# Attention and a gated feed-forward layer: other PSUM banks behind an attention burst, and two sums and one row sum in other places

## The chip, the cores and the metric

The kernel runs on one core of a Trainium2 chip. The metric is the device time of one execution in microseconds (us). The engines are called as the profile calls them: PE (TensorE: matmuls; its weight loads are listed as PEld), DVE (VectorE), ACT (ScalarE), POOL (GpSimd) and SP (which issues most transfers).

## The reference

Attention runs within chunks of 64 tokens, and its output is the input of a gated feed-forward layer:

```python
scores = scale * np.matmul(q_c, k_c.transpose(0, 1, 2, 4, 3))
scores = scores - np.max(scores, axis=-1, keepdims=True)
attn = np.exp(scores)
attn = attn / (np.sum(attn, axis=-1, keepdims=True) + 1e-09)
out = np.matmul(attn, v_c)
...
x = np.ascontiguousarray(attn_out.transpose(0, 2, 1, 3)).reshape(B * S, H * D)
g = x @ w_gate
silu = g * (1.0 / (1.0 + np.exp(-g)))
val = x @ w_val
return (silu * val @ w_out).astype(np.float32)
```

There are 8 batches, 8 heads, 576 tokens and head size 64, so x is 4608 x 512; w_gate and w_val are 512 x 1536, w_out is 1536 x 512. All arrays are float32.

## The kernel before

The 4608 tokens are nine blocks of 512. Three blocks are worked off one by one while the weights are prepared. The other six go in three pairs of blocks (`for b in range(3, NB, 2)` at the end of the function), and the change touches these pairs alone. Each float32 operand is held as a rounded upper part and a remainder, so a product of two operands is three matmuls.

**A pair** has two stages. The first is `gated_steps`: twelve steps, one for each 128 columns of the hidden layer (f = 0 to 11). Instead of eight block products a step takes seven (`seventh`, i = 0 to 6) of prepared sums of x and of weights, each 6 matmuls of 128x128 by 128x512. They go to three PSUM banks: `ps1` takes products 0, 2, 4 and 6 one on top of the other, `ps2` takes 1 and 5, `ps3` takes 3. ACT copies ps1 and ps2 out after products 0, 1 and 2 (to `h`, `v2`, `v1`), DVE adds later states of the banks to them (`add(h, ps3)`, `add(v2, ps1)` after product 4, `add(v1, ps2)`), ACT applies Silu, DVE multiplies. `Left` splits the result for the output product. Product 6 may only start when `add(v2, ps1)` has read ps1, since it adds to the same bank; the Silu of `h2` reads ps1 after product 6. Between products 5 and 6 stand the matmuls of `turns`: the output product of the step before, in four parts of 2, 1, 2 and 1 matmuls.

**The second stage** is `seven_products`: 15 units k of 12 matmuls that multiply sums of the hidden rows by sums of w_out. Before each unit, `before_unit(k)` issues on ACT the rounding of a sum (`U(k)`, line 1337) and on DVE the remainder (`L(k)`, line 1341); PE's unit k waits for them. DVE also finishes output blocks there (`finish`, lines 1399 and 1388) and works on the next pair's x (`n.s1`, `n.s4`, `n.s2`, lines 1173, 1180 and 1184, and `XL`, line 1353).

**Bursts.** While a pair runs, the attention of the next pair's two blocks is done inside its steps: at the end of steps 1 and 5 the scores of one block (`scores`, 64x64 matmuls, line 324), of steps 8 and 10 the products with v (`cross`, line 409). A burst fills four banks, two of pool `ps_gv` and then two of pool `ps_a`. The last pair has no next one and no bursts.

**Banks.** `ps_a` and `ps_gv` have two banks each, handed out in turn: a new tile gets the bank that was handed out the longest time ago and waits for its last reader. `ps_o` has four, which hold the pair's output products. In a step of the kernel before, ps1 is of `ps_a`, ps2 and ps3 are of `ps_gv`.

**Order.** PE, ACT and DVE run their instructions in the order in which the code is written; each takes the next only when what it waits for is there. Semaphores are set by the framework.

Lines behind a name are those of the kernel before.

Of the kernel before, what the change touches and what calls it, by code (L numbers as in the profile page):

```python
# [8 lines left out]
F32 = mybir.dt.float32  # L9
# [8 lines left out]
P = 128  # L18
# [6 lines left out]
NF = DF // P  # L25
# [8 lines left out]
def attn_then_gated_ffn(ctx: ExitStack, tc: tile.TileContext, qk, v, wgv, wo, out):  # L34
# [36 lines left out]
    def put_back(ps):  # L71
        return ps.rearrange("p (b a) -> p a b", a=2)

    def in_halves(x):
        return x.rearrange("p (a b) -> p a b", a=2)
# [602 lines left out]
    class Couple:  # L678
# [63 lines left out]
        def U(self, q):  # L742
            upper(self.a, self.bank(2, None), q)
# [380 lines left out]
    def scores(a, beside_pair=True, at=None, tiles=None, first=0):  # L1124

        if not tiles:
            tiles = [a.load_qk(0, 2, const, at)] if at else [a.load_qk(0), a.load_qk(1)], [a.load_qk(2, 2, const, a.at)]
        if first:
            ps2 = a.products(tiles[1], pool=ps_gv, tag="ps_gv")
            ps = a.products(tiles[0]), ps2  # L1130
        elif beside_pair:
            ps = a.products(tiles[0]), a.products(tiles[1], pool=ps_gv, tag="ps_gv")
        else:
            ps = a.products(tiles[0], pool=ps_gv, tag="ps_gv"), a.products(tiles[1])
        s = a.take(ps[0], 0)
        if beside_pair:
            a.less_top(ps[1], 2)
        a.less_top(s, 0)
        if not beside_pair:
            a.less_top(ps[1], 2)  # L1140
# [275 lines left out]
    def gated_steps(pair, middle, mid, behind, bursts, nothing=lambda: None):  # L1416
        for f in range(NF):
            for g in range(f + (f > 0), min(f + 2, NF)):
                w = hp.tile([P, 2, HM], F32R, name="left", tag=("h", "o_sb")[g % 2])
                nc.sync.dma_start(out=w.bitcast(F32), in_=two_o[g // 2][:, g % 2, :, :HM])  # L1420
                lefts[g] = w
            ps1 = ps_a.tile([P, N], F32, name="ps_a", tag="ps_a")
            ps2 = ps_gv.tile([P, N], F32, name="ps_gv")
            ps3 = ps_gv.tile([P, N], F32, name="ps_gv")
            h, h2 = pair.row(0, f), pair.row(1, f)
            v12 = const.tile([P, 2, N], F32, name="v", tag=("ts", "wo1")[f % 2])
            v1, v2 = v12[:, 0], v12[:, 1]
            seventh(ps1, pair.x, loaded[f], 0, True)
            nc.scalar.copy(out=in_halves(h), in_=put_back(ps1))
            seventh(ps2, pair.x, loaded[f], 1, True)  # L1430
            nc.scalar.copy(out=in_halves(v2), in_=put_back(ps2))
            seventh(ps1, pair.x, loaded[f], 2, False)
            nc.scalar.copy(out=in_halves(v1), in_=put_back(ps1))
            middle.get(f, nothing)()
            if f == NF - 1:
                pair.upper(1)
                pair.lower(1)
            seventh(ps3, pair.x, loaded[f], 3, True)
            if f not in value_first:
                add(h, ps3)  # L1440
            seventh(ps1, pair.x, loaded[f], 4, False)
            add(v2, ps1)
            if f in value_first:
                add(h, ps3)
            nc.scalar.activation(h, h, AF.Silu, scale=2.0 ** -8)  # L1445
            seventh(ps2, pair.x, loaded[f], 5, False)
            add(v1, ps2)
            times(h, v1)
            left = Left(pair, f, h, lefts[f])
            mid.get(f, nothing)()  # L1450
            left.lower()
            turns([0] if f in bursts else range(T))
            if f == NF - 1:
                pair.s2_of(0)
            seventh(ps1, pair.x, loaded[f], 6, False)
            nc.scalar.activation(in_halves(h2), put_back(ps1), AF.Silu, scale=2.0 ** -8)  # L1456
            times(h2, v2)
            if f in bursts:
                ahead_of_burst = [1] if f < 8 else []
                turns(ahead_of_burst)  # L1460
                bursts[f]()
                turns([t for t in (1, 2, 3) if t not in ahead_of_burst])
            behind.get(f, nothing)()
            for at, what, j in ((8, pair.s3, 0), (8, pair.s3, 1), (9, pair.s1_of, 0), (10, pair.s1_of, 1), (10, pair.s3, 2)):
                if f == at:
                    what(j)
            pending.append((left, None))
            if f + 2 < NF:
                load_weights(f + 2)
            elif f == NF - 2:  # L1470
                pair.load_sums(0)
                pair.load_sums(1)
                pair.upper(0)
                pair.lower(0)
            else:
                pair.load_sums(2)
                pair.load_sums(3)

    def seven_products(pair, n):

        loaded.clear()
        ps1, ps3 = pair.banks[0], pair.banks[1]
        ps2 = [ps_gv.tile([P, N], F32, name="ps_gv") for _ in range(2)]
        c22 = const.tile([P, 2, N], F32, name="c", tag="ts")
        c12 = const.tile([P, 2, N], F32, name="c", tag="wo1")
        c11 = [hp.tile([P, N], F32, name="c", tag="o_sb") for _ in range(2)]
# [31 lines left out]
        def before_unit(k):  # L1518
            if k == 0:
                pair.s1_of(2)  # L1520
                U(2), pair.s2_of(1), L(2), U(3), pair.s2_of(2), L(3)
            elif k == 1:
                U(4), pair.s4_of(0), L(4)
            elif k == 2:
                U(5), pair.s4_of(1), L(5)
                each(snapshot, c11, ps1)
            elif k == 3:
                U(6), pair.s4_of(2), L(6)
                each(finish(0, 0), c11, ps3)
            elif k == 4:  # L1530
                each(snapshot, c22, ps2)
                U(7), L(7), XU(0), call("s1")
            elif k == 5:
                U(8), L(8), XL(0), XU(1), call("s4")
            elif k == 6:
                each(snapshot, c12, ps1)
                U(9), L(9), call("s2"), XL(1)
            elif k == 7:
                U(10), L(10), XU(2)
            elif k == 8:  # L1540
                U(11), L(11), XL(2), XU(6)
            elif k == 9:
                U(12)
                each(finish(0, 1), c12, ps2)
                L(12)
            elif k == 10:
                U(13), L(13), XL(6)
            elif k == 11:
                U(14), XU(3), L(14), XL(3)
            elif k == 12:  # L1550
                each(snapshot, c21, ps1)
                XU(4)
                each(finish(1, 1), c22, ps1)
                call("s5"), XL(4)
# [134 lines left out]
    for b in range(3, NB, 2):  # L1689
        n, middle, mid, behind, bursts = None, {}, {}, {}, {}  # L1690
        if b + 2 < NB:
# [6 lines left out]
            def behind_factors(f, what):  # L1698
                with tc.issue_after(given[f]):
# [1 line left out]

            bursts = {1: lambda: scores(c, tiles=(q0, q2), first=2), 5: lambda: behind_factors(5, lambda: scores(n.second(), first=2)),
                      8: lambda: cross(c, first=2), 10: lambda: cross(n.a[1], first=2)}
            middle = {2: lambda: c.exponents(0, NP), 6: lambda: n.a[1].exponents(0, NP)}
            mid = {3: turned(c, 0, 1), 4: turned(c, 3, 1), 5: turned(c, 6, 1), 6: turned(c, 7, 1),
                   7: lambda: turn_some(n.a[1], 0, 1), 8: lambda: turn_some(n.a[1], 2, 1), 9: lambda: turn_some(n.a[1], 5, 1)}
            behind = {2: lambda: c.normalize(0, NP), 3: turned(c, 1, 2), 4: turned(c, 4, 2),
# [44 lines left out]
```

## Time and profile before

| what | value |
| --- | --- |
| median of 3 runs | 845.51 us (844.75 to 846.48) |
| the profiled execution | 845.21 us, of which the span from first to last instruction is 843.3 us |
| PE busy | 822.9 us, 98% of the span |
| DVE busy | 656.0 us, 78% |
| ACT busy | 438.1 us, 52% |
| POOL busy | 100.7 us, 12% |
| DMA | 217.51 MB, mean 258 GB/s |
| first pair, from 318.77 to 498.37 us | 179.60 us |
| second pair, from 498.37 to 675.77 us | 177.40 us |
| third pair, from 675.77 to the end | 167.53 us |

Times in the profile are us from the span's start. A row of a timeline is one instruction or a run of equal ones (xN), with its start and how long it lasts; in brackets stand how long the engine had been idle before it and who ended that. Matmuls overlap in the pipeline, so a run's duration reaches some tenths of a us into the next row; the distance between starts is the pace.

### The profile page before, as it was taken

To read this page: it belongs to the slowest core of one execution; us is meant where nothing else is said; L and a number is where in the kernel's file an instruction comes from. 1 tells how busy PE (TensorE), PEld (TensorE's weight loads), DVE (VectorE), ACT (ScalarE), POOL (GpSimd) and SP (SyncE) were. 2 spreads that over 40 slices of the span, in tenths; PEclk is the share of its full clock that TensorE was granted. 3 is DMA by queue.
4 is the path that set the end of the run, shared out by engine and by line. 5 is a ranking of instruction groups with operands and counts; after the bars stand their busy time and mean duration, and the time that the engine had idled before them with its cause. 6 is when DMAs were issued, how large, how long until landed. Compare 5 with 4: busy or idle time off the path is not lost.

```text
span 843.3 us, 14878 instructions
## 1 busy us (share of the span) xinstructions
PE 822.9 (98%) x5910; PEld 707.5 (84%) x5910; DVE 656.0 (78%) x944; ACT 438.1 (52%) x600; POOL 100.7 (12%) x94
## 2 busy tenths in 40 slices
PE   7999999999999999999999999999999999999998
PEld 5788788788888888888888888888878788888887
DVE  5987989867788774798997996888969963435696
ACT  4978899862614344635425644435445633333462
POOL 2100000000057673414300000000000000000000
PEclk9999999999999999999999999999999999999999
DMA  9967679799899796699976786687646866656563
GB/s 325 342 258 267 249 260 358 296 347 341 291 373 372 229 322 227 223 331 288 302 232 231 242 281 195 235 282 229 197 165 232 285 199 203 199 208 208 205 209 80
DMA packets 126949, 217.51 MB, mean 258 GB/s; under 512 B 56736, under 2 KB 88096, under 8 KB 116896
## 3 DMA queue, kind: packets, MB, share of 16 engines
q1 hardware_dynamic: 124560, 213.68, 74.3%
q10 hardware_dynamic: 2320, 2.88, 1.0%
q8 instruction: 47, 0.77, 0.4%
q14 instruction: 22, 0.18, 0.1%
HBM read 166.72 MB, written 49.81 MB: 257 GB/s over the span
## 4 chain that ended last, share of the span: by engine, by line
PE 68%; DVE 16%; DMA 6%; ACT 5%; issue 3%; SPq 1%; DVEq 0%; ACTq 0%
PE ps_a L933 21%; PE ps_gv L933 15%; PE ps_o L1298 10%; PE ps_gv L518 9%; DMA raw<-in_wgv 4%; PE ps_o L586 3%; PE ps_o L587 3%; PE ps_o L588 3%; DVE halves L1341 2%; PE ps_gv L1298 2%; DVE turned L396 2%; PE ps_a L324 2%; DMA w<-w 2%; DVE rows L1315 1%; PE ps_a L409 1%
## 5 line engine op out<-in xcount | busy, mean ns | idle before, releaser
L933 PE MATMUL ps_a<-x,factors 128*128 128x512 f32 x864 | 206.8, 380 | 2.7 <-ACT halves L1337 1.5
L933 PEld LDWEIGHTS ps_a<-x,factors 128*128 128x128 f32 x864 | 162.5, 189 | 28.3 <-DVE v L938 2.4
L933 PE MATMUL ps_gv<-x,factors 128*128 128x512 f32 x648 | 157.7, 379 | 0.0
L933 PEld LDWEIGHTS ps_gv<-x,factors 128*128 128x128 f32 x648 | 122.3, 189 | 17.8 <-DVE s_sb L340 0.5
L518 PE MATMUL ps_gv<-xh,w 128*128 128x512 f32 x320 | 94.0, 380 | 0.2 <-DVE w L157 0.2
L396 DVE STREAM_TRANSPOSE turned<-s_sb 32x256 f32<-32x256 f32 x192 | 83.6, 436 | 2.7
L1298 PE MATMUL ps_o<-halves,sums 128*128 128x512 f32 (+1 forms) x324 | 70.5, 375 | 3.0 <-PE ps_o L1298 1.8
L1298 PEld LDWEIGHTS ps_o<-halves,sums 128*128 128x128 f32 x324 | 59.7, 189 | 12.9 <-DVE halves L1341 2.8
L518 PEld LDWEIGHTS ps_gv<-xh,w 128*128 128x128 f32 x320 | 60.3, 189 | 8.9 <-DVE w L157 0.5
L557 DVE SCALAR_TENSOR_TENSOR rows<-v,rows 128x512 f32<-128x512 f32 x72 | 52.1, 723 | 14.2 <-ACT rows L1456 5.3
L1445 ACT ACTIVATE rows<-rows 128x512 f32<-128x512 f32 x36 | 22.7, 632 | 77.6 <-DVE rows L938 77.6
L518 PE MATMUL ps_gv<-xl,w 128*128 128x512 f32 x160 | 59.2, 383 | 1.3 <-ACT h L550 0.7
L1298 PE MATMUL ps_o<-hh,left 128*128 128x512 f32 x216 | 55.3, 383 | 0.0
L1280 ACT CAST hh<-rows 128x512 fp32r<-128x512 f32 x36 | 22.3, 618 | 63.4 <-DVE rows L557 63.4
L586 PE MATMUL ps_o<-both,hh 128*128 128x512 f32 (+1 forms) x151 | 55.0, 372 | 0.0
L587 PE MATMUL ps_o<-both,hh 128*128 128x512 f32 x144 | 54.6, 379 | 0.0
L588 PE MATMUL ps_o<-both,hh 128*128 128x512 f32 x144 | 54.6, 379 | 0.0
L938 DVE TENSOR_TENSOR rows<-rows,ps_gv 128x512 f32<-128x512 f32 x36 | 24.6, 683 | 37.1 <-PE ps_gv L933 36.9
L1341 DVE TENSOR_TENSOR halves<-rows,halves 128x1024 fp32r<-128x1024 f32 x36 | 43.0, 1215 | 10.4 <-ACT halves L1337 10.1
L938 DVE TENSOR_TENSOR v<-v,ps_a 128x512 f32<-128x512 f32 x44 | 30.1, 684 | 23.6 <-PE ps_a L933 23.6
L1298 PE MATMUL ps_gv<-halves,sums 128*128 128x512 f32 x216 | 48.1, 379 | 0.0
L1337 ACT CAST halves<-rows 128x1024 fp32r<-128x1024 f32 x36 | 37.1, 1049 | 19.0 <-DVE rows L1315 9.4
(171 smaller groups left out, 1391.1 us busy)
## 6 DMA issues: line engine op xcount, KB each, us to landing
factors<-t SPq DMA_DIRECT2D x36, 1024.0 KB, 6.9
factors<-w SPq DMA_DIRECT2D x36, 512.0 KB, 4.4
w<-w SPq DMA_DIRECT2D x16, 1024.0 KB, 7.8
sums<-s SPq DMA_DIRECT2D x15, 1024.0 KB, 4.9
qk_t<-in_qk SPq DMA_DIRECT2D x26, 512.0 KB, 7.9
t<-th SPq DMA_DIRECT2D x24, 512.0 KB, 4.0
raw<-in_wgv SPq DMA_DIRECT2D x11, 1024.0 KB, 6.8
both<-o SPq DMA_DIRECT2D x22, 512.0 KB, 6.3
```

Of the source, the lines that this page charges most:

```text
L396: nc.vector.transpose(out=self.turned[to:to + 32, p:p + 2, j, :, 32 * (i % 2):32 * (i % 2) + 32], in_=src[32 * i:32 * i + 32, :, o // 2, 3 ...
L518: nc.tensor.matmul(ps, w, by_turns(x), start=first and (k, i) == which[0], stop=last and (k, i) == which[-1])
L557: nc.vector.scalar_tensor_tensor(out=h, in0=v, scalar=2.0 ** -8, in1=h, op0=ALU.mult, op1=ALU.mult)
L586: nc.tensor.matmul(o[:, at], hl[:, ts], by_turns(woh)[:, at.start // 2:at.stop // 2], start=f == a.steps[0], stop=False)
L587: nc.tensor.matmul(o, hh[:, ts], by_turns(wol), start=False, stop=False)
L588: nc.tensor.matmul(o, hh[:, ts], by_turns(woh), start=False, stop=f == a.steps[1])
L933: nc.tensor.matmul(ps, w[u][:, k], by_turns(x[i][v][:, k]), start=first and k == 0 and n == 0, stop=k == NK // 2 - 1 and n == 2, skip_grou ...
L938: nc.vector.tensor_tensor(out=t, in0=t, in1=put_back(ps), op=ALU.add)
L1298: nc.tensor.matmul(to, w[:, i, u], by_turns(a[:, at]), start=first and n == 0, stop=n == 2, skip_group_check=True)
L1337: nc.scalar.copy(out=t[:, 0], in_=src)
L1341: nc.vector.tensor_tensor(out=lo, in0=src, in1=hi.bitcast(F32), op=ALU.subtract)
L1445: nc.scalar.activation(h, h, AF.Silu, scale=2.0 ** -8)
```

## The change

Four things change, all in the three pairs.

1. In a step behind a burst (f = 2, 6, 9 and 11 of the first two pairs) ps1 and ps2 come from `ps_gv` and ps3 from `ps_a`. In the first two pairs the units 0 to 2 and 6 to 8 of the second stage use `ps_a` instead of `ps_gv`.
2. In the bursts with scores, ACT copies the two `ps_gv` banks out (they are filled first) and DVE subtracts the maxima straight from the two `ps_a` banks; before it was the other way round.
3. `n.s1` and `n.s4`, the first two sums for the next pair's x, leave `before_unit(4)` and `before_unit(5)` and go to step 11, behind ACT's copy to `v1`; `U(1)` goes one place forward on ACT there.
4. `s1_of(0)`, a sum of rows, leaves the end of step 9 and goes into step 10, ahead of `left.lower()`. In steps 8 and 10 the second part of `turns` goes ahead of the burst.

```diff
@@ scores
+        if first:
+            s = a.take(ps[1], 2)
+            a.less_top(ps[0], 0)
+            a.less_top(s, 2)
+            return
         s = a.take(ps[0], 0)
@@ gated_steps
-            ps1 = ps_a.tile([P, N], F32, name="ps_a", tag="ps_a")
-            ps2 = ps_gv.tile([P, N], F32, name="ps_gv")
-            ps3 = ps_gv.tile([P, N], F32, name="ps_gv")
+            banks = (lambda: ps_a.tile([P, N], F32, name="ps_a", tag="ps_a")), (lambda: ps_gv.tile([P, N], F32, name="ps_gv"))
+            ps1, ps2, ps3 = (banks[i]() for i in ((1, 1, 0) if f - 1 in bursts else (0, 1, 1)))
...
+            if f == NF - 1:
+                pair.upper(1)
             seventh(ps1, pair.x, loaded[f], 2, False)
             nc.scalar.copy(out=in_halves(v1), in_=put_back(ps1))
             middle.get(f, nothing)()
             if f == NF - 1:
-                pair.upper(1)
                 pair.lower(1)
...
             mid.get(f, nothing)()
+            if f == NF - 2:
+                pair.s1_of(0)
             left.lower()
...
-                ahead_of_burst = [1] if f < 8 else []
+                ahead_of_burst = [1]
...
-            for at, what, j in ((8, pair.s3, 0), (8, pair.s3, 1), (9, pair.s1_of, 0), (10, pair.s1_of, 1), (10, pair.s3, 2)):
+            for at, what, j in ((8, pair.s3, 0), (8, pair.s3, 1), (10, pair.s1_of, 1), (10, pair.s3, 2)):
@@ seven_products
-        ps2 = [ps_gv.tile([P, N], F32, name="ps_gv") for _ in range(2)]
+        ps2 = [ps_a.tile([P, N], F32, name="ps_a", tag="ps_a") if n else ps_gv.tile([P, N], F32, name="ps_gv") for _ in range(2)]
...
-                U(7), L(7), XU(0), call("s1")
+                U(7), L(7), XU(0)
-                U(8), L(8), XL(0), XU(1), call("s4")
+                U(8), L(8), XL(0), XU(1)
@@ the pairs
-            middle = {2: lambda: c.exponents(0, NP), 6: lambda: n.a[1].exponents(0, NP)}
+            middle = {2: lambda: c.exponents(0, NP), 6: lambda: n.a[1].exponents(0, NP), 11: lambda: (n.s1(), n.s4())}
```

How the rows move is shown for the first pair; the second pair's rows move alike. On DVE, from the end of step 9 (the transposes) to the sum of step 11's first result, the kernel before has these rows (L938 are the three `add`s of a step, L557 the products with `h` and `h2`, L1283 is `left.lower()`, L1315 are sums of rows, L1341 are L(0) and L(1)):

```order
L396 STREAM_TRANSPOSE turned<-s_sb 32x2x4x32 x8
L1315 TENSOR_TENSOR rows<-rows 128x1024
L938 TENSOR_TENSOR rows<-rows,ps_gv 128x512
L938 TENSOR_TENSOR v<-v,ps_a 128x512
L938 TENSOR_TENSOR v<-v,ps_gv 128x512
L557 SCALAR_TENSOR_TENSOR rows<-v,rows 128x512
L1283 TENSOR_TENSOR hh<-rows,hh 128x512
L557 SCALAR_TENSOR_TENSOR rows<-v,rows 128x512
L1315 TENSOR_TENSOR rows<-rows 128x1024 x2
L1341 TENSOR_TENSOR halves<-rows,halves 128x1024 x2
L938 TENSOR_TENSOR rows<-rows,ps_gv 128x512
```

The changed kernel has these in the same place (L1320 is the line of the sums of rows there, L1288 that of `left.lower()`, L1346 that of L(k), L1178 and L1185 are those of `n.s1` and `n.s4`):

```order
L396 STREAM_TRANSPOSE turned<-s_sb 32x2x4x32 x8
L938 TENSOR_TENSOR rows<-rows,ps_gv 128x512
L938 TENSOR_TENSOR v<-v,ps_a 128x512
L938 TENSOR_TENSOR v<-v,ps_gv 128x512
L557 SCALAR_TENSOR_TENSOR rows<-v,rows 128x512
L1320 TENSOR_TENSOR rows<-rows 128x1024
L1288 TENSOR_TENSOR hh<-rows,hh 128x512
L557 SCALAR_TENSOR_TENSOR rows<-v,rows 128x512
L1320 TENSOR_TENSOR rows<-rows 128x1024 x2
L1346 TENSOR_TENSOR halves<-rows,halves 128x1024
L1178 TENSOR_TENSOR sum<-s_sb 128x1024
L1185 TENSOR_TENSOR s_sb<-s_sb 128x1024
L1346 TENSOR_TENSOR halves<-rows,halves 128x1024
L938 TENSOR_TENSOR rows<-rows,ps_a 128x512
```

One sum of rows now stands behind the three `add`s of step 10 and their product, and the two sums for the next x stand between L(0) and L(1) of step 11. In the second stage the kernel before has, on DVE, for the units 4 to 8:

```order
L1341 TENSOR_TENSOR halves<-rows,halves 128x1024
L1173 TENSOR_TENSOR sum<-s_sb 128x1024
L1341 TENSOR_TENSOR halves<-rows,halves 128x1024
L1353 TENSOR_TENSOR x<-s_sb,x 128x1024
L1180 TENSOR_TENSOR s_sb<-s_sb 128x1024
L1341 TENSOR_TENSOR halves<-rows,halves 128x1024
L1184 TENSOR_TENSOR s_sb<-sum,s_sb 128x1024
L1353 TENSOR_TENSOR x<-sum,x 128x1024
```

The changed kernel, for the same units:

```order
L1346 TENSOR_TENSOR halves<-rows,halves 128x1024 x2
L1358 TENSOR_TENSOR x<-s_sb,x 128x1024
L1346 TENSOR_TENSOR halves<-rows,halves 128x1024
L1189 TENSOR_TENSOR s_sb<-sum,s_sb 128x1024
L1358 TENSOR_TENSOR x<-sum,x 128x1024
```

Two rows of 128x1024 are gone from there, and what followed them stands two rows earlier. On PE the rows behind a burst of the first pair are, with the buffers' numbers, in the kernel before (the first row is the burst's last matmul, `hh,left` are `turns`, then products 0 to 5 of step 6):

```order
L324 MATMUL ps_a_4083<-qk_t_4044 64x64
L1298 MATMUL ps_o_3586<-hh_3927,left_3783 128x512 x3
L933 MATMUL ps_a_4147<-x_3094,factors_3966 128x512 x6
L933 MATMUL ps_gv_4148<-x_3228,factors_3969 128x512 x6
L933 MATMUL ps_a_4147<-x_3292,factors_3969 128x512 x6
L933 MATMUL ps_gv_4149<-x_3295,factors_3966 128x512 x6
L933 MATMUL ps_a_4147<-x_3350,factors_3969 128x512 x6
L933 MATMUL ps_gv_4148<-x_3413,factors_3966 128x512 x6
```

In the changed kernel:

```order
L324 MATMUL ps_a_4083<-qk_t_4044 64x64
L1303 MATMUL ps_o_3586<-hh_3927,left_3783 128x512 x3
L933 MATMUL ps_gv_4147<-x_3094,factors_3966 128x512 x6
L933 MATMUL ps_gv_4148<-x_3228,factors_3969 128x512 x6
L933 MATMUL ps_gv_4147<-x_3292,factors_3969 128x512 x6
L933 MATMUL ps_a_4149<-x_3295,factors_3966 128x512 x6
L933 MATMUL ps_gv_4147<-x_3350,factors_3969 128x512 x6
L933 MATMUL ps_gv_4148<-x_3413,factors_3966 128x512 x6
```

PE's work and its order are the same; products 0, 2 and 4 have changed places with product 3 in the pools. The next step then has its product 1 in the bank of 4147, the bank that step 6's Silu of `h2` reads last.

## Rows read from the trace of the kernel before

**Rows 1.** Timeline of PE, second stage of the first pair: start, us, instruction

```profile
465.18 7.93 PE L1298 MATMUL ps_o<-halves,sums 128*128 128x512 f32 x36
472.95 7.93 PE L1298 MATMUL ps_gv<-halves,sums 128*128 128x512 f32 x36
480.79 2.86 PE L1298 MATMUL ps_o<-halves,sums 128*128 128x512 f32 x12
484.19 5.45 PE L1298 MATMUL ps_o<-halves,sums 128*128 128x512 f32 x24 [0.55 <-DVE halves L1341]
490.53 8.01 PE L1298 MATMUL ps_o<-halves,sums 128*128 128x512 f32 x36 [0.88 <-PE ps_o L1298]
```

**Rows 2.** Windows, both second stages: length, busy us (xcount) of PE, PEld, DVE, ACT, POOL; clock, DMA

```profile
456.12:498.37 42.25, 40.82 (x187) 34.91 (x186) 41.98 (x43) 23.41 (x28) 0.00 (x0) 1.00 0.86 278
633.15:675.77 42.62, 41.04 (x187) 34.82 (x186) 42.19 (x43) 23.55 (x29) 0.00 (x0) 1.00 0.78 256
```

**Rows 3.** Timeline of DVE, second stage of the first pair

```profile
474.99 1.21 DVE L1173 TENSOR_TENSOR sum<-s_sb 128x1024 f32<-128x1024 f32 x1
...
482.93 2.35 DVE L1341 TENSOR_TENSOR halves<-rows,halves 128x1024 fp32r<-128x1024 f32 x2
...
489.22 2.33 DVE L1341 TENSOR_TENSOR halves<-rows,halves 128x1024 fp32r<-128x1024 f32 x2
```

**Rows 4.** Timeline of PE, step 10 of the first and of the second pair

```profile
439.86 0.59 PE L1298 MATMUL ps_o<-hh,left 128*128 128x512 f32 x2
441.17 1.56 PE L933 MATMUL ps_a<-x,factors 128*128 128x512 f32 x6 [0.71 <-DVE v L938]
...
616.43 1.56 PE L933 MATMUL ps_a<-x,factors 128*128 128x512 f32 x6 [0.23 <-DVE v L938]
```

**Rows 5.** Timeline of DVE, end of step 9 to step 11 of the first pair

```profile
438.70 1.23 DVE L1315 TENSOR_TENSOR rows<-rows 128x1024 f32<-128x1024 f32 x1
...
440.44 0.68 DVE L938 TENSOR_TENSOR v<-v,ps_a 128x512 f32<-128x512 f32 x1
...
443.19 0.69 DVE L1283 TENSOR_TENSOR hh<-rows,hh 128x512 fp32r<-128x512 f32 x1 [0.68 <-ACT hh L1280]
...
451.41 1.22 DVE L1341 TENSOR_TENSOR halves<-rows,halves 128x1024 fp32r<-128x1024 f32 x1 [3.30 <-ACT halves L1337]
```

**Rows 6.** Timeline of PE, behind the burst of step 5 of the first pair

```profile
387.27 0.92 PE L1298 MATMUL ps_o<-hh,left 128*128 128x512 f32 x3
...
390.90 1.46 PE L933 MATMUL ps_a<-x,factors 128*128 128x512 f32 x6
```

**Rows 7.** Timeline of PE, start of step 11 of the second pair

```profile
622.72 1.53 PE L933 MATMUL ps_a<-x,factors 128*128 128x512 f32 x6 [1.54 <-ACT halves L1337]
```

**Rows 8.** Timeline of ACT, step 2 of the first and of the second pair

```profile
349.11 1.91 ACT L345 ACTIVATE s_sb<-s_sb 128x2048 f32<-128x2048 f32 x1
...
354.59 0.59 ACT L1456 ACTIVATE rows<-ps_a 128x512 f32<-128x512 f32 x1
...
531.31 0.59 ACT L1456 ACTIVATE rows<-ps_a 128x512 f32<-128x512 f32 x1
```

**Rows 9.** Timeline of PE, step 3 of the first and of the second pair

```profile
354.77 1.46 PE L933 MATMUL ps_gv<-x,factors 128*128 128x512 f32 x6
...
362.95 2.86 PE L933 MATMUL ps_a<-x,factors 128*128 128x512 f32 x12 [0.25 <-DVE v L938]
...
531.84 1.46 PE L933 MATMUL ps_gv<-x,factors 128*128 128x512 f32 x6
```

**Rows 10.** Timeline of ACT, end of step 10 of the second pair

```profile
619.11 2.05 ACT L412 COPY s_sb<-ps_a 128x512 f32<-128x512 f32 x4 [0.20 <-PE ps_a L409]
621.04 1.07 ACT L1337 CAST halves<-rows 128x1024 fp32r<-128x1024 f32 x1
```

**Rows 11.** DMA from 619.5 to 622.5 us by queue and kind: packets, MB, share

```profile
q8 instruction: 1, 0.02, 1.9%
```

**Rows 12.** Timeline of DVE, the last subtraction of step 2 of the first pair

```profile
346.93 1.06 DVE L340 TENSOR_TENSOR s_sb<-s_sb,top 128x512 f32<-128x512 f32 x1
```

## The prediction

> **What bounds the kernel now.** I read the page first (PE busy nearly all of the span), then PE's timeline through the pairs. PE's rows there follow each other at one pace: 36 matmuls of 512 columns start at 465.18 and the next run at 472.95, so a matmul costs 7.77/36 = 0.216 us [rows 1]. The change takes no matmul away, so it can win only where PE leaves that pace. I therefore laid PE's starts against the pace through the first two pairs, and looked at each break for the instruction that ended it. There are three kinds of breaks that the change touches.
>
> *The second stage.* It has 186 matmuls (180 of units, 6 of `turns`), worth 186 x 0.216 = 40.1 us, but takes 42.25 and 42.62 us [rows 2]; 2.1 and 2.5 us are lost. In the first pair the losses stand at two places: unit 9 starts at 480.79 and unit 10 could start 12 x 0.216 later, at 483.38, but starts at 484.19 (0.81 lost); units 10 and 11 would end at 489.37, but unit 12 starts at 490.53 (1.16 lost) [rows 1]. Unit 10 waits for L(10), the first of two rows that start at 482.93, unit 12 for L(12), which starts at 489.22 [rows 3]; the second break names PE itself as the releaser, but L(12) ends right at it. DVE is busy 41.98 of 42.25 us and 42.19 of 42.62 [rows 2]: it is a queue without holes, and PE waits for its place in the queue.
>
> *Step 10.* Product 6 could start two matmuls after 439.86, at 440.29, and starts at 441.17: 0.88 lost, of which 0.71 shows as idle. It waits for `add(v2, ps1)`, which starts at 440.44, and this stood behind the sum of rows that starts at 438.70 [rows 4, 5]. The second pair shows 0.23 idle; with the same 0.17 beside it, 0.40 lost [rows 4].
>
> *Behind the bursts.* In step 6 of the first pair 3 + 12 matmuls stand between 387.27 and 390.90: 3.63 us for 3.24, so 0.39 lost [rows 6]. And product 0 of step 11 of the second pair starts at 622.72 after 1.54 idle [rows 7]; with the 0.17 again, 1.7 lost.
>
> **The change, part by part.**
>
> *`n.s1` and `n.s4` leave the second stage.* Two such operations back to back last 2.35 where one lasts 1.22, so in a queue each costs 1.13 [rows 3]; two are 2.26 us of DVE less. DVE then has 41.98 - 2.26 = 39.7 us of work against PE's 40.1, so PE bounds the stage. Unit by unit: L(10) would end 2.26 earlier than at 484.15, at 481.9, 1.5 before unit 10 wants it. L(12) would start at 486.96 and end at 488.2; unit 12 wants it at 480.79 + 36 x 0.216 = 488.56. The margin is 0.4 us, so the whole loss goes in the first pair, 2.0 us with a tenth left for restarts. In the second pair, 2.5 lost, the same 2.26 us is just enough; I take 2.2. If ACT's roundings or the snapshots held DVE up in place of its own queue, half of this would stay: low end 2.1 for both pairs, high end 4.5, value 4.2.
>
> *They enter step 11.* There DVE sits idle for 3.30 us before L(1), waiting for U(1) on ACT [rows 5]. 2.26 us fit into it, and U(1) goes a place forward, so L(1) starts earlier than before. Behind them wait L(1) and the three `add`s; price nothing. Without the cover they would cost 2.26 us of DVE in step 11, and product 6 there would wait for most of it; that is the bound, and the hole of 3.30 excludes it. U(1) now stands before the copy to `v1`, which delays that by about a third of a rounding; product 4, which needs ps1 read, comes a whole product (1.3 us) behind. Nothing.
>
> *`s1_of(0)` moves to step 10.* `add(v2, ps1)` starts 1.13 earlier, at 439.3, and ends 0.3 before product 6 wants it. The moved sum now stands before `left.lower()`, where DVE was idle for 0.68 anyway, waiting for ACT [rows 5]; the rest, some 0.5 us, delays the remainder, which is used only in the next step. Gain: 0.88 + 0.40 = 1.3 us, unless something later in the step takes it (below).
>
> *Other banks behind a burst.* Product 0 and 1 now use banks that ACT copies out while the burst's second half runs; product 3, 3.9 us later, uses a bank that DVE has read by then. That takes away most of the 0.39 us of step 6 [rows 6]; the three other steps behind score bursts and the ones behind `cross` show less. I take 0.7 in all (0 to 0.9).
>
> *What the new banks make late.* In the step after, product 1 now sits in the bank that Silu of `h2` reads last. In step 2 that Silu starts at 354.59 and ends at 355.18; product 1 of step 3 starts at 354.77 [rows 8, 9]. It will wait 0.45 us. In the first pair that is mostly taken from a wait that exists already: product 6 of step 3 starts at 362.95 with 0.25 idle, waiting for DVE, whose time hangs on the same Silu [rows 9]. In the second pair the Silu ends at 531.90 and product 1 starts at 531.84 [rows 8, 9]: 0.1. Steps 7 I take like the latter. Cost 0.4 (0.2 to 0.8).
>
> *The rest* (score copies swapped between ACT and DVE, one matmul of `turns` ahead of two bursts, banks of units 0 to 2 and 6 to 8) changes neither the amount of work nor a wait that the trace shows: the cover is DVE's slack ahead of the exponent. Nothing; without the cover some 0.6 us in each of four steps, my estimate of the half burst by which DVE now begins later.
>
> *The 1.7 us of step 11.* The profile puts it to the rounding U(0). That rounding starts at 621.04 and ends at 622.11, 0.6 us before PE goes on, and product 0 does not read what it writes; the copies that free its bank, four from 619.11, end at 621.16 [rows 7, 10]. Elsewhere PE follows its releaser by 0.05 us: `add(v2, ps1)` ends at 441.12, product 6 starts at 441.17 [rows 4, 5]. So I don't believe the name. What else goes on there: one block of instructions is loaded [rows 11], right after a burst of 128 small matmuls that eats instructions fast. My reading is that PE's sequencer had nothing to run. Then other banks don't help: the 1.7 us stay, and arriving 0.4 earlier only makes PE wait 0.4 longer; in the first pair, where PE now comes 0.88 earlier to the same place and did not wait before, I take 0.3 lost (0 to 0.88).
>
> The Trainium skill speaks against this reading (Runtime: NRT & Kernel Launch, section Instruction fetch mechanics): instructions are fetched ahead in 16 KiB blocks over a queue of their own, and crossing a block is, in its words, "mostly hidden". The block size agrees with the trace's packet (0.02 MB); that it is hidden is what the gap in step 11 puts in doubt, and if the page holds here, the first rival below is the case.
>
> **Sum.** 4.2 + 1.3 + 0.7 - 0.4 - 0.7 (the 0.4 and 0.3 at step 11) = 5.1 us. The profiled execution took 845.21, 0.30 under the median of 845.51. From the median: 845.5 - 5.1 = **840.4 us**. A measurement of this kernel tells about 0.2% (1.7 us) from no change, so that is faster.
>
> **Rivals.**
>
> *The wait in step 11 is one for the bank, as the profile names it.* Then ps1 from `ps_gv`, free after the first two copies, ends it: 1.7 more but for a tenth, and the 0.7 is not taken back. 4.2 + 1.3 + 0.7 - 0.4 + 1.6 = 7.4, so 838.1 us. For it speaks the name in the profile, against it the 0.6 us between the rounding's end and the start. The load could also simply come earlier this time, with the same result. Chance 0.25.
>
> *The second stage gives back half.* DVE's queue is short of 2.26 us, but PE is only 2.1 and 2.5 behind; if L(12) or the output's `finish` comes up against ACT, the transfers or the snapshots, the margin of 0.4 is gone and unit 12 waits as before. 845.5 - 3.0 = 842.5 us. For it: the margin is small. Against it: DVE's rows show no hole that a wait for ACT would leave [rows 2]. Chance 0.15.
>
> *Slower: the Silu in front of product 1.* In four steps (3 and 7 of two pairs) PE now hangs on ACT's chain exponent, Silu, rounding, Silu of `h2`. The exponent of step 2 starts at 349.11, and DVE's subtractions, which end at 347.99 [rows 8, 12] and now begin half a burst later (put at 0.6 us), must be done before it: the slack is 0.5 us. Each us by which DVE is later than that goes through exponent and Silu to product 1. It needs 5.1 + 1.7 us over four steps, so a delay of some 1.7 us each beyond the slack; then 847.2 or more. Against it: nothing in DVE's queue grows there. Chance 0.03.
>
> *No change:* PE's gaps reappear elsewhere in the pairs, within 1.7 us of before. Since PE alone has full work after the gaps go, and the first two pairs have 340 us of it with few other breaks, I give 0.07.
>
> The forecast's own chance is 0.5. Its range is 839.0 to 841.8 from the bounds of the parts. With the first two rivals, the range for 8 in 10 is 837.4 to 843.2. Faster by over 0.2%: 0.5 + 0.25 + 0.15 = 0.90; within: 0.07; slower: 0.03.
>
> **What would show it.** In the changed kernel's profile: units 10 and 12 start without idle time and both second stages take 40.2 to 40.4 us; DVE has holes in them; product 6 of step 10 has no wait for `add(v2, ps1)`; DVE's idle time in step 11 before L(1) shrinks to under 1 us; product 1 of step 3 in the first pair waits for a Silu. If step 11 of the second pair still shows 1.5 to 2.2 us of idle PE, with a bank that was long free, the load of instructions is the cause; if it shows none, the first rival is right. Wrong would make the prediction above all a DVE that is late in step 11 for another reason, so that units 0 to 3 wait.

## The result and the profile after

| kernel | median us (runs) | the profiled execution | span |
| --- | --- | --- | --- |
| before | 845.34 (4) | 845.21 | 843.3 |
| changed | 836.31 (4: 834.96, 835.89, 839.61, 836.73) | 834.96 | 833.2 |

The ratio is 0.9897 [0.9866, 0.9928]: 8.7 us shorter by the ratio, 9.0 by the medians. Timed twice more, the changed kernel took 837.21 and 836.25 us at ratios of 0.9893 [0.9879, 0.9907] and 0.9893 [0.9879, 0.9908]. That is 4.1 us faster than the forecast's 840.4, 2.7 us under its own range (from 839.0) and 1.1 us under the range for 8 in 10 (from 837.4).

**Where the time came from.** I laid PE's starts against its pace in both kernels again. The first two pairs last 347.86 us (from 317.76 to 665.62) instead of 357.00; that is 9.1 of the 10.1 us between the two spans. The other 1.0 us lies ahead of the pairs (the burst of step 1 starts at 339.22 in place of 340.23), where nothing was changed; in a second profile of the changed kernel it starts at 339.51, in others of kernels with the same opening between 339.16 and 341.35. This 1.0 us lies within that scatter, so I don't count it as a gain.

The second stage of the first pair, PE's timeline after:

```profile
462.26 7.93 PE L1303 MATMUL ps_o<-halves,sums 128*128 128x512 f32 x36
470.03 7.93 PE L1303 MATMUL ps_a<-halves,sums 128*128 128x512 f32 x36
477.80 15.70 PE L1303 MATMUL ps_o<-halves,sums 128*128 128x512 f32 x72
493.34 1.46 PE L933 MATMUL ps_a<-x,factors 128*128 128x512 f32 x6
```

Units 9 to 14 are one row of 72 matmuls; in [rows 1] they were three rows, with breaks ahead of units 10 and 12. Both stages by windows (length, then busy us of PE, PEld, DVE, ACT, POOL):

```profile
453.19:493.34 40.15, 40.15 (x188) 35.15 (x186) 39.88 (x41) 23.75 (x28) 0.00 (x0) 1.00 0.87 277
625.47:665.62 40.15, 40.15 (x188) 35.13 (x187) 39.88 (x41) 23.76 (x28) 0.00 (x0) 1.00 0.81 259
```

Beside 42.25 and 42.62 in [rows 2] that is 2.10 and 2.47 us: 4.57. PE is now busy for all of the stage. DVE's work fell by 2.1 and 2.3 us and still fills all but 0.27 us, so the two engines are nearly level.

Steps 10 and 11 of the first pair on PE:

```profile
437.39 0.59 PE L1303 MATMUL ps_o<-hh,left 128*128 128x512 f32 x2
437.82 1.46 PE L933 MATMUL ps_a<-x,factors 128*128 128x512 f32 x6
439.12 0.38 PE L1303 MATMUL ps_o<-hh,left 128*128 128x512 f32 x1
439.43 2.10 PE L409 MATMUL ps_a<-turned,v_t 64*64 64x64 f32 x128
441.45 0.92 PE L1303 MATMUL ps_o<-hh,left 128*128 128x512 f32 x3
442.20 1.67 PE L933 MATMUL ps_gv<-x,factors 128*128 128x512 f32 x7
444.24 1.99 PE L933 MATMUL ps_gv<-x,factors 128*128 128x512 f32 x8 [0.36 <-issue]
```

Product 6 (437.82) follows the two matmuls of `turns` at the pace; the 0.88 us of [rows 4] are gone, and in the second pair the 0.39. But a new break stands at 444.24, in the middle of a product: seven matmuls take 1.51 us, so 0.52 are lost, and the profile names no releaser ("issue"). In the second pair the same place has none, where [rows 7] had 1.54 idle and 1.7 lost (PE, second pair):

```profile
614.36 0.92 PE L1303 MATMUL ps_o<-hh,left 128*128 128x512 f32 x3
615.11 3.19 PE L933 MATMUL ps_gv<-x,factors 128*128 128x512 f32 x14
```

DVE in the first pair shows that the moved work stands where it had been idle [rows 5]; from L(0) at 443.65 to `add(h, ps3)` at 448.33 it has no pause:

```profile
436.94 0.68 DVE L938 TENSOR_TENSOR v<-v,ps_a 128x512 f32<-128x512 f32 x1
...
443.65 1.22 DVE L1346 TENSOR_TENSOR halves<-rows,halves 128x1024 fp32r<-128x1024 f32 x1
444.79 1.22 DVE L1178 TENSOR_TENSOR sum<-s_sb 128x1024 f32<-128x1024 f32 x1
446.04 1.23 DVE L1185 TENSOR_TENSOR s_sb<-s_sb 128x1024 f32<-128x1024 f32 x1
447.19 1.23 DVE L1346 TENSOR_TENSOR halves<-rows,halves 128x1024 fp32r<-128x1024 f32 x1
448.33 0.68 DVE L938 TENSOR_TENSOR rows<-rows,ps_a 128x512 f32<-128x512 f32 x1
```

Behind the burst of step 5 (PE, first pair) the 3 + 18 matmuls take 4.64 us to the next row for 21 x 0.216 = 4.54, so 0.1 is lost where [rows 6] showed 0.39:

```profile
385.17 0.92 PE L1303 MATMUL ps_o<-hh,left 128*128 128x512 f32 x3
385.93 4.05 PE L933 MATMUL ps_gv<-x,factors 128*128 128x512 f32 x18
389.81 0.38 PE L933 MATMUL ps_a<-x,factors 128*128 128x512 f32 x1
```

The largest single part of what the forecast missed therefore lies in step 11: 1.7 us are gone where it kept them. Two questions follow. Is that wait one for a bank (the first rival) or for instructions? And if for instructions, why did it go?

### The profile page after: what moved, and what is told of

Its sections match the earlier page's. It is cut to its first block, busy times and chain, and to the rows that moved or that the text cites. A ratio compares the mean times of both kernels' runs of the same rounds, so it can differ in the third digit from the quotient of the medians.

```text
span 833.2 us, 14881 instructions
## 1 busy us (share of the span) xinstructions
PE 818.9 (98%) x5910; PEld 708.5 (85%) x5910; DVE 654.0 (79%) x944; ACT 438.6 (53%) x600; POOL 99.5 (12%) x94
## 4 chain that ended last, share of the span: by engine, by line
PE 82%; DVE 7%; ACT 6%; DMA 2%; issue 2%; SPq 0%; DVEq 0%; ACTq 0%
PE ps_gv L933 21%; PE ps_a L933 19%; PE ps_o L1303 14%; PE ps_gv L518 9%; PE ps_a L1303 4%; PE ps_o L586 3%; PE ps_o L587 3%; PE ps_o L588 3%; PE ps_a L324 2%; PE ps_gv L1303 2%; PE ps_a L409 1%; ACT t L105 1%; ACT wo L105 1%; DVE t L116 1%; DVE w L157 1%
## 5 line engine op out<-in xcount | busy, mean ns | idle before, releaser
L933 PE MATMUL ps_gv<-x,factors 128*128 128x512 f32 x792 | 188.9, 379 | 0.4 <-issue 0.4
L933 PE MATMUL ps_a<-x,factors 128*128 128x512 f32 x720 | 171.9, 379 | 0.0
L933 PEld LDWEIGHTS ps_gv<-x,factors 128*128 128x128 f32 x792 | 149.5, 189 | 22.1 <-issue 0.8
L933 PEld LDWEIGHTS ps_a<-x,factors 128*128 128x128 f32 x720 | 136.0, 189 | 19.4
L557 DVE SCALAR_TENSOR_TENSOR rows<-v,rows 128x512 f32<-128x512 f32 x72 | 51.3, 713 | 13.5 <-ACT rows L1450 5.3
L938 DVE TENSOR_TENSOR rows<-rows,ps_gv 128x512 f32<-128x512 f32 x28 | 19.1, 683 | 36.1 <-PE ps_gv L933 35.9
L938 DVE TENSOR_TENSOR v<-v,ps_gv 128x512 f32<-128x512 f32 x52 | 35.5, 685 | 15.2 <-PE ps_gv L933 15.2
L1303 PEld LDWEIGHTS ps_o<-hh,left 128*128 128x128 f32 x216 | 40.2, 189 | 5.9
L1346 DVE TENSOR_TENSOR halves<-rows,halves 128x1024 fp32r<-128x1024 f32 x36 | 42.7, 1213 | 1.1 <-ACT halves L1342 1.0
```

The lines of the kernel that those rows point to most:

```text
L557: nc.vector.scalar_tensor_tensor(out=h, in0=v, scalar=2.0 ** -8, in1=h, op0=ALU.mult, op1=ALU.mult)
L933: nc.tensor.matmul(ps, w[u][:, k], by_turns(x[i][v][:, k]), start=first and k == 0 and n == 0, stop=k == NK // 2 - 1 and n == 2, skip_grou ...
L938: nc.vector.tensor_tensor(out=t, in0=t, in1=put_back(ps), op=ALU.add)
L1303: nc.tensor.matmul(to, w[:, i, u], by_turns(a[:, at]), start=first and n == 0, stop=n == 2, skip_group_check=True)
L1346: nc.vector.tensor_tensor(out=lo, in0=src, in1=hi.bitcast(F32), op=ALU.subtract)
```

## The experiments

### One part of the change alone

Four kernels: the kernel before with one part of the change, and one with two. They ran on one chip; the kernel before took 844.99 us there (22 runs).

Only the sums, `n.s1` and `n.s4` with `U(1)`:

```diff
+            if f == NF - 1:
+                pair.upper(1)
...
-                pair.upper(1)
...
-                U(7), L(7), XU(0), call("s1")
+                U(7), L(7), XU(0)
-                U(8), L(8), XL(0), XU(1), call("s4")
+                U(8), L(8), XL(0), XU(1)
...
-            middle = {2: ..., 6: ...}
+            middle = {2: ..., 6: ..., 11: lambda: (n.s1(), n.s4())}
```

> The kernel before, with n.s1 and n.s4 (and U(1)) in step 11 and nothing else changed. Theory (DVE's queue): both second stages fall from 42.25 and 42.62 us to 40.1 to 40.4, units 10 and 12 start without a wait, and the kernel is 4.3 to 4.6 us shorter: 840.8 us beside 845.3. Rival (half comes back, since L(1) or the adds of step 11 come later and the margin of unit 12 is gone): about 2 us shorter, with a wait before unit 12 still there or a new one at product 6 of step 11. The gap before product 0 of step 11 of the second pair (1.7 us) stays by either theory of that gap, since banks and instruction count are those of before.

Measured: 840.85 us, ratio 0.9950 [0.9931, 0.9968]. The windows of both second stages:

```profile
454.26:494.56 40.30, 40.30 (x187) 34.98 (x186) 39.88 (x41) 23.77 (x29) 0.00 (x0) 1.00 0.84 268
628.75:668.88 40.13, 40.13 (x187) 35.15 (x186) 39.85 (x41) 23.75 (x28) 0.00 (x0) 1.00 0.81 259
```

The whole gain of the second stages comes with this part, and product 6 of step 11 shows no new wait: the theory of DVE's queue holds, its rival falls. The gap of step 11 of the second pair stays, at 1.19 us.

Only the sum of rows:

```diff
+            if f == NF - 2:
+                pair.s1_of(0)
             left.lower()
...
-            for at, what, j in (..., (9, pair.s1_of, 0), (10, pair.s1_of, 1), ...):
+            for at, what, j in (..., (10, pair.s1_of, 1), ...):
```

> The kernel before, with s1_of(0) moved to step 10 and nothing else changed. Both theories: product 6 of step 10 loses no time, 0.88 us in the first pair and 0.40 in the second. If the gap in step 11 is a late load of instructions, PE meets it earlier: the gap of the second pair is 1.7 to 2.1 us and the first pair may show a new one of up to 0.5; the kernel is 0.4 to 1.3 us shorter. If it is a bank that ACT frees late, the gap stays 1.7 and the first pair shows none: 1.3 shorter, 844.0 us.

Measured: 842.17 us, 0.9968 [0.9956, 0.9980], 2.7 us shorter and so over both expectations. Product 6 of step 10 has no wait in either pair, as both theories had it. But the gap of the second pair neither stays 1.7 nor grows: it is gone, with the banks of the kernel before. The first pair has a new one of 0.61 us:

```profile
444.47 1.46 PE L933 MATMUL ps_a<-x,factors 128*128 128x512 f32 x6
445.77 0.38 PE L933 MATMUL ps_gv<-x,factors 128*128 128x512 f32 x1
446.60 1.24 PE L933 MATMUL ps_gv<-x,factors 128*128 128x512 f32 x5 [0.45 <-issue]
...
618.90 1.13 PE L1298 MATMUL ps_o<-hh,left 128*128 128x512 f32 x4
619.86 1.46 PE L933 MATMUL ps_a<-x,factors 128*128 128x512 f32 x6
```

Only the banks, the score copies and `turns`:

```diff
-            ps1 = ps_a.tile(...)
-            ps2 = ps_gv.tile(...)
-            ps3 = ps_gv.tile(...)
+            banks = (lambda: ps_a.tile(...)), (lambda: ps_gv.tile(...))
+            ps1, ps2, ps3 = (banks[i]() for i in ((1, 1, 0) if f - 1 in bursts else (0, 1, 1)))
...
-                ahead_of_burst = [1] if f < 8 else []
+                ahead_of_burst = [1]
...
```

> The kernel before, with the order of banks, the swapped score copies and the one part of turns ahead of the bursts changed, and the sums left in place. If the gap of 1.7 us before product 0 of step 11 of the second pair is a wait for the bank, it is gone here, and with 0.7 behind the other bursts the kernel is about 2.4 us shorter (842.9). If it is a late load of instructions, a gap of 1 to 2 us stays there although its bank is long free, or it goes only where the load itself is seen to land at least 1 us earlier; without that the kernel is 0.3 to 0.7 us shorter (844.8). The second stages stay at 42.2 to 42.7 us.

Measured: 844.08 us, 0.9986 [0.9973, 0.9999]. PE at the start of step 11 of the second pair:

```profile
619.49 0.48 PE L1303 MATMUL ps_o<-hh,left 128*128 128x512 f32 x1
621.52 0.59 PE L1303 MATMUL ps_o<-hh,left 128*128 128x512 f32 x2 [1.55 <-issue]
621.95 2.32 PE L933 MATMUL ps_gv<-x,factors 128*128 128x512 f32 x10
```

The gap is still there (1.81 us lost) and has moved two matmuls forward, between two matmuls of one `turns` group that use a bank of `ps_o` already held. A wait for the bank of product 0 can't stand there. With this the first rival's mechanism falls.

The sums and the row sum together, banks as before:

> The changed kernel with the banks, the score copies and turns as before. By the terms taken singly (second stages 4.5, step 10 1.3) and nothing taken back it is 5.8 us shorter, 839.5 us. If instructions load late, 0.3 to 0.9 of that is lost before product 0 or inside product 1 of step 11, so 839.8 to 840.4. If the banks are worth more than the 0.7 of the forecast (the changed kernel took 836.3), this kernel lies 3 us or more over it.

Measured: 838.26 us, 0.9917 [0.9896, 0.9937], 7.0 us shorter. The parts alone give 4.2, 2.7 and 1.2 us by their ratios, 8.1 together, and the change 9.0 [7.9, 10.2] by its repeats: they add up within what these intervals can tell. The third expectation (3 us over the changed kernel) did not come; this kernel lies 2 us over it by the ratios. In its profile gaps that name no releaser stand at three places, the largest, 1.25 us, behind the burst of step 5.

### Where such gaps stand

I counted PE's instructions (matmuls, weight loads and its few semaphore instructions) up to each gap, and looked for the packets of PE's instruction queue (q8, 16 KB each). Each profile has 47 such packets for some 12,000 instructions, one per 256. In the pairs of the 12 profiles, ten matmuls that carry no wait of their own start 0.2 us late or more; with the two gaps of step 11 that the profile puts to ACT (before, only the sums) that makes 12. All 12 stand at an instruction whose number leaves 193 to 195 when divided by 256: 9923 in the kernel before, 7362 in the changed one. And PE goes on 1.3 to 1.7 us after a packet of q8 has landed:

| kernel, pair | product 6 of step 10 starts | transfers take 80% of the DMA engines from about | packet of q8 | PE goes on | lost |
| --- | --- | --- | --- | --- | --- |
| before, first | 441.17 | 441.2 | 444.16 to 445.10 | no gap | 0 |
| before, second | 616.43 | 617.1 | 620.14 to 621.07 | 622.72 | 1.71 |
| only the sums, second | 612.62 | 613.0 | 616.05 to 616.93 | 618.39 | 1.19 |
| only the banks, second | 615.76 | 616.3 | 619.26 to 620.23 | 621.52 | 1.81 |
| only the row sum, second | 615.36 | 616.5 | 615.89 to 617.17 | no gap | 0 |
| only the row sum, first | 439.97 | 441.1 | 444.38 to 445.34 | 446.60 | 0.61 |
| changed, first | 437.82 | 438.8 | 441.87 to 442.83 | 444.24 | 0.52 |
| changed, second | 610.73 | 612.0 | 611.36 to 612.27 | no gap | 0 |

The transfers are the first two of `sums<-s`, 1 MB each, issued behind products 5 and 6 of step 10. Where the packet comes ahead of them it starts 0.5 to 0.6 us behind the start of product 6; where they come first, 3.0 to 4.4 us. In the second pair it is a race between two transfers that some tenths of a us turn: where the large transfers come 0.4 to 0.7 us behind product 6 the packet comes last, where they come 1.1 to 1.3 us behind it the packet is ahead. In the first pair they come first in all three rows. There the kernel before has no gap because PE reaches that instruction only at 447.27, 2.2 us after the packet has landed.

### Let the block of instructions go first

If that is right, holding the transfers back must end the gap, with banks, instructions and their order as they were.

```diff
+    burst_end = []
...
-                nc.scalar.copy(out=self.s[:, p:p + n, :, j], in_=px[j])
+                burst_end.append(nc.scalar.copy(out=self.s[:, p:p + n, :, j], in_=px[j]).ins)
...
-                nc.sync.dma_start(out=w[:, m:n].bitcast(F32), in_=kept_s[:, 4 * t + m:4 * t + n])
+                d = nc.sync.dma_start(out=w[:, m:n].bitcast(F32), in_=kept_s[:, 4 * t + m:4 * t + n]).ins
+                if t < 2 and burst_end:
+                    tc.add_manual_dep(d, burst_end[-1].name, ...Sync...)
```

> The kernel before, with the first two transfers of sums<-s of the second stage held back until ACT has copied out the burst of step 10 (a wait on the queue alone; banks, instructions and their order stay). Theory (a block of instructions lands late because these transfers fill the DMA engines from 616.9 us on): the block starts within 1.5 us of product 6 of step 10 instead of 3.7 us behind it, and the 1.7 us before product 0 of step 11 of the second pair are gone; 843.2 us beside 845.0. Rival (ACT frees the bank late): the gap stays, since the copies of the burst end when they did; 845.0. A cost is possible in unit 0 of the second stage, if its sums land after 633 us: they have about 10 us for 5.6.

Measured: 844.09 us beside 845.55, 0.9985 [0.9973, 0.9997]. The DMA queues between 616.9 and 620.1 us (packets, MB, share), before:

```profile
q1 hardware_dynamic: 146, 1.10, 88.4%
```

and with the transfers held back, where product 6 starts at 616.41 and so within 0.02 us of before:

```profile
q8 instruction: 1, 0.02, 1.8%
```

The packet lands at 617.58 to 618.52, and PE goes through step 11 at the pace:

```profile
620.03 1.13 PE L1300 MATMUL ps_o<-hh,left 128*128 128x512 f32 x4
621.00 1.46 PE L935 MATMUL ps_a<-x,factors 128*128 128x512 f32 x6
```

This is shown, then: the wait was there because 1 MB transfers lay in front of something that PE needed, and the packet of instructions is what now comes earlier. That it was the instructions and nothing else behind these transfers, the shifted kernels below show. The second stages lost nothing (42.28 us in the first pair beside 42.25).

The same in the changed kernel, for the 0.52 us of the first pair, and the changed kernel itself beside it:

> The changed kernel with the first two transfers of sums<-s held back until ACT has copied out the burst of step 10. Theory (late block): the block of the first pair starts within 1.5 us of product 6 of step 10 instead of 4.2 us behind it, the 0.52 us in product 1 of step 11 are gone in the first pair, the second pair keeps having none; 0.3 to 0.8 us shorter than the changed kernel, 836.3 us beside 845.4. Rival (that gap has another cause, since it names no semaphore): the 0.52 us stay.

> The changed kernel a third time, for its scatter beside the one with held-back transfers: 836 to 838 us, with the 0.3 to 0.6 us gap in product 1 of step 11 of the first pair in the profile and none in the second pair.

Measured: 836.89 us (0.9899 [0.9881, 0.9917]) with held-back transfers, 836.25 without; the kernel before took 844.95. In the profiles the gap is there without (0.53 us) and gone with them; PE, first pair, with held-back transfers:

```profile
443.69 0.92 PE L1305 MATMUL ps_o<-hh,left 128*128 128x512 f32 x3
444.45 3.83 PE L935 MATMUL ps_gv<-x,factors 128*128 128x512 f32 x17
```

The half us is under what these four runs each can show. With nothing in its way the packet starts 1.12 us behind product 6 in the first pair and 0.46 in the second. In the changed kernel the large transfers come 1.0 and 1.3 us behind product 6, so the first pair loses the race and the second wins it.

### Move the ends of the blocks

The other half of the theory is that the place of a gap is set by the count of instructions. 32 transposes whose result nobody reads, 64 instructions, stand behind the first matmuls of the opening (in the kernel before this also swaps two stores with a load on SP in the first pair):

```diff
         for _ in range(n):
             nc.tensor.matmul(ps, ident, ...)
+        for _ in range(32):
+            nc.tensor.transpose(ps[:C, 0, :C], ident[:C, :C], ident[:C, :C])
```

> The kernel before, with 32 transposes of 64x64 (64 instructions of PE) behind the first matmuls of the opening, whose result nobody reads; the pairs are those of before. Theory (blocks of 256 instructions): every place at which PE can run out of instructions comes 64 instructions earlier in the pairs, well ahead of the bursts, so no step of the pairs shows a gap without a semaphore, the 1.7 us of step 11 are gone, and no new one of over 0.3 us comes; 843.3 us plus 0 to 1.2 for the transposes in the opening. Rival (bank): the gap of 1.7 us stays where it is.

> The changed kernel with the same 32 transposes in the opening. Theory (blocks): the gap of 0.52 us in product 1 of step 11 of the first pair is gone and no other appears; 0.5 us shorter than the changed kernel, plus 0 to 1.2 for the transposes, and the runs lie closer together than 834.96 to 839.61. Rival: the gap stays.

> The changed kernel once more, on the chip of the other three: 836.3 us again within 1.5 us. By the theory of the late block any gap without a semaphore lies at the same place of a block as the 0.52 us of step 11, or two blocks apart from it, and its size varies from run to run with the transfers.

Measured: the kernel before so shifted 844.57 us beside 845.55 (0.9985 [0.9973, 0.9997]), the changed one 837.67 beside 837.21. Neither profile has such a gap anywhere in the pairs; product 0 of step 11 of the second pair of the kernel before follows at the pace:

```profile
621.93 1.13 PE L1300 MATMUL ps_o<-hh,left 128*128 128x512 f32 x4
622.89 1.46 PE L935 MATMUL ps_a<-x,factors 128*128 128x512 f32 x6
```

The large transfers are still there, with 80% of the DMA engines from 0.5 us behind product 6 on, so they did not hold up anything but instructions. The changed kernel without the shift has its 0.52 us again, at instruction 7362 again. The first burst of the pairs starts at 342.26 and 341.28 us in the two shifted kernels; as it starts between 339.16 and 341.35 in the ten profiles without the shift, what the transposes cost is not shown. That the runs would lie closer together is not borne out: 836.66 to 842.18.

## Why the prediction was wrong, step by step

**The range.** The bounds of the parts do not give 839.0 to 841.8. The lower end takes the best of each part and nothing at step 11 (4.5 + 1.3 + 0.9 - 0.2 = 6.5 us); with the worst of each, 2.1 + 1.3 + 0 - 0.8 - 1.3 = 1.3 us, the upper end would have been 844.2. No bound let the 1.7 us of step 11 go; only the first rival did.

**The second stages: right.** 4.2 forecast, 4.57 measured; the margin of 0.4 us of unit 12 held in both pairs. "DVE has holes" was hardly so: 39.88 us of work, not 39.7.

**Step 10: right.** 1.3 forecast, 0.88 + 0.39 measured.

**The sums in step 11: right.** The idle 3.30 us took them.

**Banks behind the bursts: right in size.** 0.7 forecast. With this part alone PE loses some 1.0 us less in the steps of the two pairs (without the break inside the burst of step 5, below, and that of product 6 of step 3), and 0.2 more ahead of product 6 of step 10.

**The wait of product 1 for the Silu of `h2`: wrong.** I put -0.4; there is none. In the second profile of the changed kernel product 1 of step 3 (first pair) starts ahead of that Silu. PE, then ACT:

```profile
353.95 1.46 PE L933 MATMUL ps_gv<-x,factors 128*128 128x512 f32 x6
```

```profile
354.00 0.59 ACT L1463 ACTIVATE rows<-ps_gv 128x512 f32<-128x512 f32 x1
```

The Silu reads its bank of `ps_gv` while product 1 writes, and the trace has product 1 wait on DVE's semaphore, not on ACT's. So it does not use the bank that the Silu reads; my reading of the rotation of banks was wrong there, and so is the sentence ahead of the prediction that puts product 1 of the next step in that bank.

**The 1.7 us of step 11: the mechanism right, the step behind it wrong.** That PE "had nothing to run" is shown. The failed step is "the 1.7 us stay, and arriving 0.4 earlier only makes PE wait 0.4 longer". It took the arrival of the block as fixed. In the second pair it is the outcome of a race with the transfers of `sums<-s`; without the wait of product 6, which the row sum alone takes away, the packet wins it (+1.7 us). In the first pair the transfers come first in either kernel, and what the step said of PE arriving earlier there came: 0.52 lost, where I took 0.3 (0 to 0.88). In place of -0.7 this term is +1.2. The first rival's outcome came by its last sentence ("the load could also simply come earlier this time"), not by its bank; I had it in the text and didn't work out what would bring it about. So the sign that I gave for telling the two apart (no idle time in step 11 means that the first rival is right) was wrong: step 11 of the second pair shows none, and the rival's mechanism is not the cause.

With these the sum is 4.6 + 1.3 + 0.8 + 1.2 = 7.9 us, beside 9.0 [7.9, 10.2] in the better timed repeats. Up to 1 us of the median is not placed.

**What differs from run to run.** Two breaks of the kernel before are in other profiles of either kernel, or not: 0.53 us inside the burst of step 5 (0.52 in the third profile of the changed kernel, 0.15 to 0.24 in most), and the one ahead of product 6 of step 3 [rows 9], 0.41 here, 0.64 and 0.67 in the two shifted kernels, 0.32 in the third profile of the changed kernel, 0.96 with the sums and the row sum. These are in the 9.1 us by which the two pairs of the two profiles differ, up to 0.9 us of it, and I don't count them to the change. The third profile of the changed kernel has one more, 0.55 us in step 8, that names DVE.

**The slower rival** did not come: steps 2, 3, 6 and 7 of the two pairs take no longer in the changed kernel than before.

## What to carry to other kernels

An idle engine for which the profile names a releaser that ended half a us earlier, or none ("issue"), may be waiting for its own instructions: count its instructions to that place, see whether such places lie a whole number of blocks apart, and look when the queue of instructions moved. If large transfers are issued just ahead of a stretch that eats instructions fast, hold them back by a wait on their queue; here, where they had slack, that cost nothing. And when a term of a forecast is a race between two transfers, an earlier arrival may as well end a wait as lengthen it: work out both sides.

## What the runs showed of the hardware

PE can run dry. The Trainium skill (Runtime: NRT & Kernel Launch, section Instruction fetch mechanics) calls the crossing of a block "mostly hidden". In the pairs that holds for all but at most three blocks of a profile, but those cost up to 1.8 us each: a burst of 128 matmuls with their weight loads takes 256 instructions, a whole block, in 2.1 us, while a packet of 16 KB behind 1 MB transfers started 3.0 to 4.4 us behind product 6 in place of 0.5 to 1.7 with nothing in its way, and PE went on only 1.3 to 1.7 us after it had landed.

DVE and POOL slow each other. In step 2 of the first pair POOL still adds sums while DVE multiplies. DVE before, then POOL before:

```profile
352.99 1.04 DVE L557 SCALAR_TENSOR_TENSOR rows<-v,rows 128x512 f32<-128x512 f32 x1 [1.21 <-ACT rows L1445]
354.71 1.26 DVE L1283 TENSOR_TENSOR hh<-rows,hh 128x512 fp32r<-128x512 f32 x1 [0.69 <-ACT hh L1280]
```

```profile
353.43 1.19 POOL L1248 TENSOR_TENSOR sums<-sums 128x256 f32<-128x256 f32 x1
354.70 0.73 POOL L1249 TENSOR_TENSOR sums<-sums 128x256 f32<-128x256 f32 x1
```

In the changed kernel's first profile, the same in that order:

```profile
351.87 0.69 DVE L557 SCALAR_TENSOR_TENSOR rows<-v,rows 128x512 f32<-128x512 f32 x1 [1.21 <-ACT rows L1450]
353.25 0.69 DVE L1288 TENSOR_TENSOR hh<-rows,hh 128x512 fp32r<-128x512 f32 x1 [0.69 <-ACT hh L1285]
```

```profile
351.08 0.73 POOL L1253 TENSOR_TENSOR sums<-sums 128x256 f32<-128x256 f32 x1
351.90 1.26 POOL L1254 TENSOR_TENSOR sums<-sums 128x256 f32<-128x256 f32 x1
```

Whichever starts some hundredths of a us later lasts half a us longer: DVE at 354.71 behind POOL at 354.70, POOL at 351.90 behind DVE at 351.87.

The Trainium skill (SBUF — State Buffer, section Who interferes with whom) names a port pair that DVE and GpSimd share. The rows agree that one holds up the other; that this makes the break at product 6 of step 3, which hangs on the same DVE queue, I have argued from its rows and not tried.
